# Two MLPs behind a retention layer: the state's product in 64x64 tiles, decays at the outputs, small loads on ScalarE's queue, one output bank in halves

## The chip, the cores and the metric

The kernel runs on one core of a Trainium2 chip. Its time is the device time of one execution in microseconds. Three runs of the kernel before gave 575.33, 578.35 and 578.90 us; the median is 578.35 us. One execution was profiled; its own time was 576.97 us.

## The reference

The program has three stages. First a retention layer over 2 sequences of 768 positions with 8 heads of 64 features, then an MLP with a rational activation, then an MLP with SiLU. Both MLPs take 1536 rows of 512 features through 2048 hidden features.

```python
gamma = 1.0 - 2.0 ** (-5.0 - np.arange(H))          # one decay per head
state = np.zeros((B, H, D, D))
for t in range(S):
    state = gamma * state + einsum('bhd,bhe->bhde', k[:, :, t], v[:, :, t])
    y[:, :, t] = scale * einsum('bhd,bhde->bhe', q[:, :, t], state)
x = y.transpose(0, 2, 1, 3).reshape(B * S, H * D)   # 1536 x 512
h = x @ w_in;   x = (P(h) / (Q(h) + 1e-6)) @ w_out  # P cubic in h, Q from |h| and h*h
h = x @ w_in2;  out = (h * sigmoid(h)) @ w_out2
```

## The kernel before, in words

**Retention in chunks.** The 1536 positions are cut into 12 chunks of 128: chunk c is piece c // 2 of sequence c % 2. A chunk has four parts on TensorE. The scores (line 472) are 8 products kT by qT with 64 rows of contraction, into two PSUM banks. VectorE masks each bank into SBUF (`am`, one 128x512 instruction a bank). The product of the masked scores with v (line 509) is 8 products with 64 output partitions. For the ten chunks that have a predecessor, the product of the state with the queries (line 519) is 4 products of 128x128: the state `bd` holds two heads of a pair in the two diagonal 64x64 blocks, the other two blocks are zero. Chunks 0 to 9 also add k by v to the state (line 497). All these operands are plain fp32, and the trace shows two records for one such product.

**Decays.** VectorE or GpSimd scales v by a falling decay (`vn`), and q by a rising one (`qT` by `gq`, line 467; `gq` is `up0` times a rate per piece). So the output of a chunk leaves PSUM as it is: ScalarE copies it to `xh`, VectorE subtracts to `xl`.

**MLPs.** Every fp32 matrix is carried as a high and a low half in fp32r (`xh` and `xl`, `ih`/`il` for w_in, `oh`/`ol` for w_out, `gh`/`gl` for the activations), and each product is three products of 128x512. A step is one block of 128 hidden features for a group of 512 rows: 12 products into a bank `h0`, `h1`, `a0` or `a1` (line 556), the activation on ScalarE and VectorE, the split into `gh` and `gl`, and 12 products into the four banks `acc0` to `acc3` (line 609). Weights come in 512 KB pieces (`raw`), which ScalarE and VectorE turn into fp32 (`wt`) and split. For one pair of groups of the second MLP seven products stand for eight (line 772). The end is 240 products of line 609 in a row for the last group; then ScalarE copies each `acc` bank to SBUF and SyncE sends it out (lines 644 and 654).

**Order.** The whole program is a list of operations with their dependencies (class `Flow`). The order in which each engine gets them is a table, `ORDER`, packed in a string. The functions fix the operations, buffers and banks; the table fixes the sequence on TensorE (PE), VectorE (DVE), ScalarE (ACT), GpSimd (POOL) and on SyncE's queue (SP). An instruction waits for the semaphores of what it depends on, and everything behind it on its engine waits too.

Of the kernel before, what the change touches and what calls it, by code (L numbers as in the profile page):

```python
# [11 lines left out]
F32 = mybir.dt.float32  # L12
# [11 lines left out]
R = {"gqd": 0, 'lw': -463.92, 'T0': 689.59, 'tau0': 13.93, 'tau1': 122.19, 'c0': -129.63, 'dc': 67.51, 'conv': 39.61, 'half': 427.29, 'absl': -34.77, 'raw': 455.03, 'ret': 752.06, 'spl': -417.39, 'hi': 301.24, 'lo': 31.56, 'inn': -277.93, 'later': -32.81, 'split': -554.53, 'out': 359.39, 'evac': -363.13, 'qload': -20.08, 'scl': 238.79, 'sc': 858.37, 'am': -44.15, 'gr': 112.48, 'av': -547.62, 'bd': 198.47, 'xh': -201.14, 'xl': 110.32, 'glp': 48, 'lop1': 24, 'lop2': 30, 'scp': 4, 'ps': 17, 'ksc': 103.89, 'qa': -467.29, 'ka': 0, 'late': 20, 'mid': 4, 'pev': -317.29, 'pld': -385.01, 'cg': -489.85, 'wm': 11, 'mk': 26.43, 'ck': 21.3, 'g2': (1, 0, 2), 'ch0': 269.21, 'ch1': -102.81, 'ch2': 64.3, 'ch3': 22.33, 'ch4': -52.46, 'ch5': 5.42, 'ch6': -78.23, 'ch7': 237.84, 'ch8': 90.06, 'ch9': -61.88, 'ch10': -106.39, 'ch11': -212.52, 'ru0': 218.22, 'lu0': -107.8, 'ru1': 40.68, 'lu1': -106.06, 'ru2': 91.09, 'lu2': 146.01, 'ru3': -37.17, 'lu3': -39.51, 'rhalf': 125.38, 'wsum': 20.0, 'kd': 4, 'hb': 20, 'turned': ()}  # L24
# [7 lines left out]
    'c-jrtW5W<;7XaXMA3xc(W!r1DW!tvB7Ps88ZQHhOn+wa@;+FNk|Ka*@eGdY0AvUB3ggEdW1OUhg=|CX?7^DRT2ZDr<2XaFOhzwC75hR9akOVTpkB',  # L32
    '}MSLoz4{Ng+DKgBVZ(qCj#;0Wl#fq=YPx7mh<INCnv-7UY8(@DuzDsUbg9hcu8K%0fXX068Ehl!Ka32Y!HDP#8`?8K?kt;T)8QlTZv!K_RFO^`JO',
    'hg)>kDN<)2U0T-YWG=T1K7S2OaxCXW0Pq+w;pgB~9>rf3Y!xi`oB88^V5E{cxh#6YK9cTkh;56KZW>66-Llt-rci|R%fKSjC9zvAR4t{~D5IOt~v',
    'BO8`0<l8W&<f&&-{1>$g-4Jew1&s<1lmInxB-8|CHNKYLkH*touMN<g+Y)s`~%$}dguxFAYO<czCtf}24%u$h!LK{_n|kufR``~qJ{6mD@Yi=!9a',
# [4 lines left out]
    'RaOjVPRp|8Fq&~FgWZ9Gs0Tf8)k)lVSi|f2f~JMF<c0j!mqd}Yz_y*<!~i5!>eI6tbuD`9sC(uVQbt1_rvvYBRmK<!^7|>ObUlW2W*4Q@o~5no`k',  # L40
    '1iE6ffp@b9oOY=gG=Hf#!A@O?NO{t3^*v2ZeMhb`e<_yybHZfKAD;Y0Woo`)UqBK#F*hBM)F*bB$QK5+aPPK1}?RX7ql;+OC>+zxlbx3Cjt<1RP=',
    'X9Hj)jKJ6b=l4DSj*;<R_%|R%!KfGw-vq)1!Eg@F#poCV6Jbk?iATe!5DS09*w_^lVq#2!NpT@A!n+|8#zDro7!Q+Sa!i5qFbgim|3XSkg_*G%rp',
    '7dw6|-XwT!M!n8!Da-oiHut#2;`icE`?m5DH*H{0;>RVJ`d;bK`PciAym77RAE20yAPdoR7tDJ;ui(_$L;}O1KIS!!am<d9Wmw!pc}0GvETOg6r@',
# [935 lines left out]
```

## Time and profile before

| | us |
|---|---|
| median of 3 runs (lowest, highest) | 578.35 (575.33, 578.90) |
| profiled execution, its own time | 576.97 |
| span of its trace | 575.2 |
| PE busy | 565.8 |
| VectorE busy | 432.8 |
| ScalarE busy | 405.9 |
| GpSimd busy | 184.5 |

The span is from the first to the last instruction of the trace. "Busy" is the time in which at least one instruction of the engine ran. PE's granted clock is given as a share of full speed (1.00 is 2.4 GHz, 0.50 is 1.2 GHz; a value between the two is a mean over a stretch). "DMA share" is the mean busy share of the 16 DMA engines. A `<-` behind an idle time names what ended it.

### The profile page before, as it was taken

How to read it: one execution, taken by the hardware profiler on the slowest of the kernel's cores; microseconds unless marked ns; L12 is line 12 of the kernel's file. 1: busy time of each engine (PE TensorE's matmuls, PEld its weight loads, DVE VectorE, ACT ScalarE, POOL GpSimd, SP SyncE). 2: the span in 40 equal slices, each digit the busy share in tenths (PEclk: the TensorE clock that was granted, in tenths of full speed). 3: DMA queues.
4: the chain of work that ended last, by engine and by line, in shares of the span. 5: the costliest groups of instructions: out<-in, count | busy, mean ns of one | idle time of the engine just before them, and what ended most of it. 6: DMA issues, size and time to landing. Idle time of an engine off the chain costs nothing.

```text
span 575.2 us, 8252 instructions
## 1 busy us (share of the span) xinstructions
PE 565.8 (98%) x2912; PEld 466.3 (81%) x2912; DVE 432.8 (75%) x680; ACT 405.9 (71%) x698; POOL 184.5 (32%) x148
## 2 busy tenths in 40 slices
PE   8989999999999999999999999999999999999997
PEld 7867878888788888888888888888888888888885
DVE  5888889788988898797988567578887888673341
ACT  2688889889999879788999877786544545424332
POOL 2556574633454634263373743310000000000000
PEclk8989999999999999999999999999999999999999
DMA  8996843632321321012134668864323422117811
GB/s 257 358 362 228 300 170 97 216 116 86 128 89 59 111 71 58 19 37 92 68 134 154 211 210 291 263 209 165 128 93 108 148 73 94 54 41 227 257 61 74
DMA packets 41441, 85.05 MB, mean 148 GB/s; under 512 B 4150, under 2 KB 4278, under 8 KB 41400
## 3 DMA queue, kind: packets, MB, share of 16 engines
q1 hardware_dynamic: 41400, 84.52, 43.1%
q8 instruction: 23, 0.38, 0.3%
q14 instruction: 18, 0.15, 0.1%
HBM read 63.53 MB, written 20.97 MB: 147 GB/s over the span
## 4 chain that ended last, share of the span: by engine, by line
PE 90%; DVE 3%; ACT 3%; DMA 2%; issue 1%; SPq 0%; POOL 0%; ACTq 0%
PE acc L609 42%; PE h L556 18%; PE a L556 10%; PE h L772 7%; PE a L772 7%; PE a L472 2%; DMA kn<-in_k_dram 1%; PE a L509 1%; PE a L519 1%; ACT h L331 1%; DVE s L346 1%; PE a L497 1%; DMA qT<-in_qt_dram 1%; DVE u L346 1%; PE h L509 1%
## 5 line engine op out<-in xcount | busy, mean ns | idle before, releaser
L339 POOL TENSOR_TENSOR gl<-s,gh 128x512 fp32r<-128x512 f32 x48 | 63.6, 1328 | 109.5 <-ACT gh L331 70.7
L609 PE MATMUL acc<-gh,oh 128*128 128x512 f32 x192 | 75.5, 393 | 0.0
L609 PE MATMUL acc<-gl,oh 128*128 128x512 f32 x192 | 74.8, 389 | 0.0
L609 PE MATMUL acc<-gh,ol 128*128 128x512 f32 x192 | 74.8, 389 | 0.0
L609 PE MATMUL acc<-oh,gh 128*128 128x512 f32 x192 | 74.7, 389 | 0.0
L609 PE MATMUL acc<-ol,gh 128*128 128x512 f32 x192 | 74.7, 389 | 0.0
L609 PE MATMUL acc<-oh,gl 128*128 128x512 f32 x192 | 74.7, 389 | 0.0
L556 PE MATMUL h<-xh,ih 128*128 128x512 f32 x168 | 66.2, 394 | 0.1
L556 PE MATMUL h<-xl,ih 128*128 128x512 f32 x168 | 65.5, 390 | 0.0
L556 PE MATMUL h<-xh,il 128*128 128x512 f32 x168 | 65.5, 390 | 0.0
L346 DVE SCALAR_TENSOR_TENSOR wt<-wt,raw 128x512 int32<-128x512 int32 x64 | 49.2, 778 | 17.1 <-ACT raw L331 13.2
L417 POOL TENSOR_TENSOR ol<-wt,oh 128x512 fp32r<-128x512 f32 x36 | 48.3, 1349 | 30.8 <-ACT oh L412 26.1
L417 POOL TENSOR_TENSOR il<-wt,ih 128x512 fp32r<-128x512 f32 x36 | 47.6, 1332 | 32.3 <-ACT ih L412 30.3
L331 ACT ACTIVATE raw<-raw,par 128x512 int32<-128x512 uint32 x64 | 48.3, 762 | 3.3 <-DMA raw<-in_moe_w_in_dram 1.7
L346 DVE SCALAR_TENSOR_TENSOR s<-s,par,h 128x512 f32<-128x512 f32 x65 | 48.2, 745 | 2.5 <-ACT w L331 1.0
L331 ACT ACTIVATE gh<-s 128x512 fp32r<-128x512 f32 x56 | 35.0, 626 | 14.2 <-DVE s L346 7.4
L331 ACT ACTIVATE wt<-raw 128x512 f32<-128x512 f32 x64 | 42.4, 664 | 3.0 <-DMA raw<-in_moe_w_out_dram 1.8
L609 PEld LDWEIGHTS acc<-gh,oh 128*128 128x128 f32 x192 | 36.0, 188 | 7.9
L609 PEld LDWEIGHTS acc<-gl,oh 128*128 128x128 f32 x192 | 36.0, 188 | 7.6
L609 PEld LDWEIGHTS acc<-oh,gl 128*128 128x128 f32 x192 | 36.0, 188 | 7.5
L609 PEld LDWEIGHTS acc<-ol,gh 128*128 128x128 f32 x192 | 36.0, 188 | 7.5
L609 PEld LDWEIGHTS acc<-oh,gh 128*128 128x128 f32 x192 | 36.0, 188 | 7.4
(263 smaller groups left out, 1301.0 us busy)
## 6 DMA issues: line engine op xcount, KB each, us to landing
raw<-in_moe_w_in_dram SPq DMA_DIRECT2D x32, 512.0 KB, 4.7
raw<-in_moe_w_out_dram SPq DMA_DIRECT2D x32, 512.0 KB, 4.7
spill<-wt SPq DMA_DIRECT2D x48, 256.0 KB, 4.5
wt<-spill SPq DMA_DIRECT2D x48, 256.0 KB, 2.9
vn<-in_v_dram SPq DMA_DIRECT2D x12, 256.0 KB, 4.2
qT<-in_qt_dram SPq DMA_DIRECT2D x12, 256.0 KB, 4.5
kT<-in_kt_dram SPq DMA_DIRECT2D x12, 256.0 KB, 4.6
kn<-in_k_dram SPq DMA_DIRECT2D x10, 256.0 KB, 4.6
```

Of the source, the lines that this page charges most:

```text
L331: lambda: nc.scalar.activation(out=out_, in_=in_, func=func, **kw),
L339: op(eng, dur, rank, lambda: e.tensor_tensor(out=out_, in0=in0, in1=in1, op=alu), reads, writes, port)
L346: lambda: nc.vector.scalar_tensor_tensor(out=out_, in0=in0, scalar=scalar, in1=in1, op0=op0, op1=op1),
L417: e.tensor_tensor(out=sl.t[nm + "l"][:, us], in0=wt.t, in1=sl.t[nm + "h"][:, us].bitcast(F32), op=ALU.subtract)
L472: nc.tensor.matmul(heads(sb_[j].t)[:, hp, :], kT.t[js, hp, :], qT.t[js, hp, :], start=True, stop=True)
L497: nc.tensor.matmul(st.t[j * D : (j + 1) * D, hp * D : (hp + 1) * D], kn.t[:, 2 * hp + j, :], vn.t[:, 2 * hp + j, :], start=(hp == 0), stop ...
L509: nc.tensor.matmul(heads(xo.t)[j * D : (j + 1) * D, hp, :], vn.t[:, 2 * hp + j, :], heads(am[j].t)[:, hp, :], start=(hp == 0), stop=not mo ...
L519: nc.tensor.matmul(heads(xo.t)[:, hp, :], old.t[:, hp, :], qT.t[:, hp, :], start=False, stop=True, skip_group_check=True,)
L556: nc.tensor.matmul(h.t, sl.t[w][:, ws], x[g].t[:, c, :], start=(n == 0), stop=(n == 3 * KD - 1))
L609: nc.tensor.matmul(a.t, a1, a2, start=(first and n == 0), stop=(last and n == 2))
L772: nc.tensor.matmul(b_.t, w[0](c, wlo), x[0](c, xlo), start=(start and n == 0), stop=(n == 5), skip_group_check=True)
```

## The change

- **State's product.** `bd` becomes 128x4x64 without zero blocks: four heads lie in partitions 0 to 63 and four in 64 to 127. The product with the queries is 8 products of 64x64 by 128 (line 523), which go round the four quarters of the array. Half of the queries lie in the other half of the partitions than their state, so GpSimd copies these into `qm` (two 64x256 copies a chunk, line 457). The two row halves write two banks, which are the chunk's own score banks.
- **Decays at the outputs.** q is no longer scaled. The output is multiplied by `up0` (piece 0) or `gq` when VectorE takes it out of PSUM into `xf` (one 128x512 instruction, or two of 128x256 for chunks with a state); ScalarE copies `xf` to `xh`. The subtraction to `xl` is VectorE's for chunks 0 to 3 and GpSimd's after that. The addition to the state is one 128x256 instruction instead of two of 64x256.
- **Small transfers.** The constants and parameters are loaded from ScalarE's queue (`beside`, 4 loads) instead of SyncE's (5 loads). Some memsets move from VectorE to GpSimd, two on GpSimd go, the identity goes, and the warming products at the start are 6 instead of 11.
- **Last bank in halves.** For the last group of the second MLP, the last step of bank `acc3` is two times three products of 256 columns, each half with its own copy and transfer.
- **Order.** `ORDER` is a new table, and the chunks are entered in the list of operations in four places instead of one; so banks and buffers can be shared in another sequence.

```diff
-R = {"gqd": 0, ..., 'wm': 11, ...}
+R = {"xp": 4, "vd": (0, 1, 2, 3), "early": ((0, 7), (2, 8), (3, 9), (4, 12)), "gqd": 0, ..., 'wm': 6, ...}
...
-    bd = [Buf(f"bd{r}", [P, HP, P], F32, at) for r in range(2)]
+    bd = [Buf(f"bd{r}", [P, HP, D], F32, at) for r in range(2)]
+    xfs = Turns("xf", 2, [P, GT], F32, at)
+    qms = Turns("qm", 2, [P, 2, P], F32, at)
-    gqs = Turns("gq", 2, [P, HP, P], F32, at)
+    gqs = Turns("gq", 1, [P, HP, P], F32, at)
...
+    def beside(rank, out_, in_, writes):
+        op("act", 0.42, rank, lambda: nc.scalar.dma_start(out=out_, in_=in_), [], writes)
...
+        if more:
+            qm = qms()
+            for r in range(2):
+                rs, js = slice(r * D, (r + 1) * D), slice((1 - r) * D, (2 - r) * D)
+                def move(out_=qm.t[rs, :, :], in_=qT.t[js, 2 * r : 2 * r + 2, :]):
+                    nc.gpsimd.tensor_copy(out=out_, in_=in_)
+                op("pool", 0.31, rank, move, [qT], [qm] if r == 0 else [qm.low])
...
-        tt("dve" if c < R["scp"] else "pool", rank - R["scl"], qT.t[:], qT.t[:], up, ALU.mult, [gq], [qT], port=more)
...
+        def place(hp, j):
+            x = xo[hp // 2 % len(xo)]
+            return heads(x.t)[j * D : (j + 1) * D, hp % 2 if len(xo) == 2 else hp, :]
...
             if more:
-                for hp in range(HP):
-                    nc.tensor.matmul(heads(xo.t)[:, hp, :], old.t[:, hp, :], qT.t[:, hp, :], ...)
+                for a in range(2):
+                    for r, j in ((0, 0), (1, 1), (0, 1), (1, 0)):
+                        hp, rs = 2 * r + a, slice(r * D, (r + 1) * D)
+                        x = qT.t[rs, hp, :] if r == j else qm.t[rs, a, :]
+                        nc.tensor.matmul(place(hp, j), state.t[rs, 2 * a + j, :], x, start=False, stop=True, skip_group_check=True)
...
-        act(rank + R["xh"], hi, heads(xo.t), AF.Copy, [xo], xh[g].chunk[o], True)
-        tt("dve", rank + R["xl"], lo, heads(xo.t), hi.bitcast(F32), ALU.subtract, [xo, *xh[g].chunk[o]], xl[g].chunk[o], port=False)
+        for n, x in enumerate(xo):
+            ks = slice(2 * n, 2 * n + 2) if more else slice(0, KD)
+            wide = 2 if more else KD
+            tt("dve", rank + R["xh"], whole[:, ks, :], heads(x.t)[:, 0:wide, :], shared[ci].t[:, ks, :], ALU.mult, [x, shared[ci]], [full], n=wide * P, port=False)
+        act(rank + R["xh"], hi, whole, AF.Copy, [full], xh[g].chunk[o])
+        tt("dve" if c < R["xp"] else "pool", rank + R["xl"], lo, whole, hi.bitcast(F32), ALU.subtract, [full, *xh[g].chunk[o]], xl[g].chunk[o])
...
+    def ends(now, g, sl, wr, cs, gh, gl, a):
+        for half in range(2):
+            hs = slice(half * GT // 2, (half + 1) * GT // 2)
...
+            op("pe", 0.36, now + R["out"], mm_end, ..., [c])
+            op("act", 0.263, now + R["evac"], lambda hs=hs: nc.scalar.activation(out=o.t[:, hs], in_=a.t[:, hs], func=AF.Copy, scale=0.5), [c], [to])
+            op("sync", 0.4, now + R["evac"], lambda hs=hs: nc.sync.dma_start(out=out[r0 : r0 + P, hs], in_=o.t[:, hs]), [to], [])
...
+            if last and l == 1 and g == gb and m == 3:
+                ends(now, g, sl, wr, cs, gh, gl, a)
+                continue
```

SyncE's queue at the start of the program, before (a name and a number are a buffer; `vn` is v, `kn` is k, both with positions in the partitions; `qT` and `kT` have features there; 88 KB `cst` holds the decays):

```order
L365 DMA vn_200<-in_v_dram 128x512
L365 DMA vn_201<-in_v_dram 128x512
L365 DMA cst<-in_consts_dram 128x176
L365 DMA qT_203<-in_qt_dram 128x512
L365 DMA t_177<-in_consts_dram 1x512
L365 DMA t_176<-in_consts_dram 1x512
L365 DMA qT_204<-in_qt_dram 128x512
L365 DMA kT_206<-in_kt_dram 128x512
L365 DMA kT_207<-in_kt_dram 128x512
L365 DMA pin<-in_moe_b_dram 1x2
L365 DMA pin<-in_moe_a_dram 1x4
L365 DMA kn_197<-in_k_dram 128x512
```

and after the change:

```order
L370 DMA qT_204<-in_qt_dram 128x512
L370 DMA kT_207<-in_kt_dram 128x512
L370 DMA vn_201<-in_v_dram 128x512
L370 DMA vn_199<-in_v_dram 128x512
L370 DMA raw_159<-in_moe_w_in_dram 128x2x512
L370 DMA vn_200<-in_v_dram 128x512
L370 DMA kT_208<-in_kt_dram 128x512
L370 DMA qT_205<-in_qt_dram 128x512
L370 DMA kT_207<-in_kt_dram 128x512
L370 DMA kn_196<-in_k_dram 128x512
```

q and k of chunk 0 now come first, the small loads are gone to ScalarE's queue (where `cst` is first), and a 512 KB piece of w_in comes fifth, ahead of k.

TensorE around the end of chunk 6, before (`a0`, `a1`, `h0` and `acc` are PSUM banks; line 497 adds to the state, 472 makes scores, 509 takes the masked scores, 519 the state):

```order
L497 MATMUL a0_184<-vn_2_202,kn_2_199 64x64 x8
L472 MATMUL a0_184<-qT_0_203,kT_0_206 128x128
...
L497 MATMUL a0_184<-vn_0_200,kn_0_197 64x64 x8
L509 MATMUL a1_185<-am0_212,vn_0_200 64x128
...
L519 MATMUL a1_185<-qT_0_203,bd0_195 128x128 x4
L556 MATMUL h0_190<-xh0_69,ih1_79 128x512
```

and after the change (494, 510, 523 and 560 are the lines that 497, 509, 519 and 556 were):

```order
L494 MATMUL acc2_187<-vn_0_199,kn_0_196 64x64 x8
L494 MATMUL acc3_188<-vn_2_201,kn_2_198 64x64 x8
L510 MATMUL a0_183<-am0_214,vn_0_199 64x128
...
L510 MATMUL a1_184<-am0_214,vn_0_199 64x128
...
L523 MATMUL a0_183<-qT_0_204,bd0_194 64x128
L523 MATMUL a1_184<-qT_0_204,bd0_194 64x128
L523 MATMUL a0_183<-qm_0_209,bd0_194 64x128
L523 MATMUL a1_184<-qm_0_209,bd0_194 64x128
...
L560 MATMUL h0_189<-xh0_68,ih1_78 128x512
```

Before, everything around chunk 6 goes through the banks `a0` and `a1`; now the additions to the state have `acc2` and `acc3`, which are still free there. In both, 24 products of the first MLP step pair and the chunks 0 to 6 lie ahead of the last row, and chunks 7 to 11 behind it.

TensorE at the very end, after the change (each bank's row stands for its last products):

```order
L609 MATMUL acc_188<-oh_84,gh_179 128x256
L609 MATMUL acc_188<-ol_85,gh_179 128x256
L609 MATMUL acc_188<-oh_84,gl_182 128x256
...
L637 MATMUL acc_187<-oh_84,gh_179 128x512
L637 MATMUL acc_187<-ol_85,gh_179 128x512
L637 MATMUL acc_187<-oh_84,gl_182 128x512
L637 MATMUL acc_185<-oh_84,gh_179 128x512
L637 MATMUL acc_185<-ol_85,gh_179 128x512
L637 MATMUL acc_185<-oh_84,gl_182 128x512
```

`acc_188` is bank `acc3`, the one in halves. Between its second half and the end stand 18 products of 512 columns; the bank that ends last is `acc0` (`acc_185`), whole, as it was before.

## Rows read from the trace of the kernel before

**Rows 1.** page part 1, busy us (share of span) and instructions of each engine

```profile
PE 565.8 (98%) x2912; PEld 466.3 (81%) x2912; DVE 432.8 (75%) x680; ACT 405.9 (71%) x698; POOL 184.5 (32%) x148
```

**Rows 2.** windows; PE, PEld, DVE, ACT, POOL busy us (instructions), PEclk, DMA share, GB/s

```profile
44.40:571.60 527.20, 527.03 (x2484) 432.96 (x2482) 398.46 (x621) 378.86 (x651) 164.81 (x126) 1.00 0.40 134
5.00:41.30 36.30, 32.19 (x387) 27.07 (x387) 30.75 (x53) 22.08 (x41) 17.18 (x16) 0.94 0.98 354
...
140.00:160.00 20.00, 19.87 (x88) 16.10 (x87) 17.46 (x25) 19.05 (x34) 7.45 (x6) 1.00 0.27 94
```

**Rows 3.** windows, same columns, around the start

```profile
35.00:40.00 5.00, 3.32 (x50) 2.73 (x44) 4.59 (x8) 3.94 (x8) 3.46 (x3) 1.00 1.04 402
40.00:45.00 5.00, 4.18 (x42) 3.84 (x43) 4.89 (x9) 4.97 (x10) 3.21 (x4) 0.66 0.42 163
```

**Rows 4.** timeline 40:45: start us, us, engine, line, tile, form, count

```profile
40.04 1.28 DVE L339 TENSOR_TENSOR am<-a,causal 128x512 f32<-128x512 f32 x2
...
41.70 1.94 PE L509 MATMUL a<-am,vn 128*64 128x128 f32 x16
...
43.58 1.16 PE L519 MATMUL a<-qT,bd 128*128 128x128 f32 x8
...
44.49 0.47 PE L556 MATMUL h<-xh,ih 128*128 128x512 f32 x1
```

**Rows 5.** chain of waits: start us, us, what (chunk 8, and the end)

```profile
84.53 1.02 PE a L509 x16
85.55 1.09 PE a L519 x8
...
516.49 54.41 PE acc L609 x240
```

**Rows 6.** PE groups by form: busy us, mean ns, idle

```profile
L519 PE MATMUL a<-qT,bd 128*128 128x128 f32 x64 | 9.3, 288 | 0.0
```

**Rows 7.** timeline: weight loads and products of 64 columns

```profile
26.27 0.55 PEld L497 LDWEIGHTS a<-vn,kn 128*64 128x64 f32 x16 [0.70 <-DMA kn<-in_k_dram]
...
26.79 0.64 PE L497 MATMUL h<-vn,kn 128*64 128x64 f32 x16
...
34.36 0.85 PEld L509 LDWEIGHTS a<-am,vn 128*64 128x64 f32 x16 [0.35 <-issue]
```

**Rows 8.** timeline 0:12, SyncE's issues and VectorE's first work

```profile
0.74 0.86 SPq L365 DMA_DIRECT2D vn<-in_v_dram  x2
1.64 0.42 SPq L365 DMA_DIRECT2D cst<-in_consts_dram  x1
...
5.00 0.69 DVE L339 TENSOR_TENSOR vn<-vn,cst 128x512 f32<-128x512 f32 x1 [3.57 <-DMA cst<-in_consts_dram]
...
8.19 1.16 PE L472 MATMUL a<-qT,kT 64*128 64x128 f32 x16 [0.78 <-DMA kn<-in_k_dram]
...
29.66 0.44 SPq L365 DMA_DIRECT2D kn<-in_k_dram  x1
```

**Rows 9.** VectorE and GpSimd groups by form: busy us, mean ns, idle

```profile
L339 DVE TENSOR_TENSOR xl<-a,xh 128x512 fp32r<-128x512 f32 x8 | 5.5, 683 | 0.1
...
L339 DVE TENSOR_TENSOR bd<-a,bd 64x256 f32<-64x256 f32 x12 | 5.0, 420 | 1.2 <-PE a L497 1.1
...
L346 DVE SCALAR_TENSOR_TENSOR wt<-wt,raw 128x512 int32<-128x512 int32 x64 | 49.2, 778 | 17.1 <-ACT raw L331 13.2 <-ACT wt L331 3.8
...
L339 POOL TENSOR_TENSOR qT<-qT,gq 128x512 f32<-128x512 f32 x8 | 10.3, 1284 | 9.2 <-DMA qT<-in_qt_dram 9.2
...
L834 POOL MEMSET bd<- 128x512 f32 x2 | 1.0, 524 | 0.3 <-POOLq L956 0.3
```

**Rows 10.** page part 6, DMA issues: count, KB each, median us to landing

```profile
kn<-in_k_dram SPq DMA_DIRECT2D x10, 256.0 KB, 4.6
```

**Rows 11.** timeline, the end of the program

```profile
571.60 0.60 ACT L644 ACTIVATE u<-acc 128x512 f32<-128x512 f32 x1
...
572.23 0.33 SPq L654 DMA_DIRECT2D out_dram<-u  x1
```

More of the change, by code (lines that the diff above doesn't have):

```diff
@@ L509, in outs @@
                     nc.tensor.matmul(
-                        heads(xo.t)[j * D : (j + 1) * D, hp, :],
+                        place(hp, j),
                         vn.t[:, 2 * hp + j, :],
                         heads(am[j].t)[:, hp, :],
-                        start=(hp == 0),
+                        start=(hp % 2 == 0 if more else hp == 0),
                         stop=not more,
@@ L528, in attention @@
         if grows:
             op("pe", 0.6, rank + R["gr"], grow, [kn, vn], [st])
-        op("pe", 1.94 if more else 0.98, rank + R["av"], outs, [vn, *am] + ([old, qT] if more else []), [xo])
+        op("pe", 1.5 if more else 0.98, rank + R["av"], outs, [vn, *am] + ([state, qT, qm, qm.low] if more else []), xo)
         if grows:
-            sv = st.t[:, 0 : HP * D].rearrange("p (a e) -> p a e", a=HP)
-            for j in range(2):
-                js = slice(j * D, (j + 1) * D)
-                if not more:
-                    act(rank + R["bd"], new.t[js, :, js], sv[js], AF.Copy, [st], [new], True, n=HP * D)
-                else:
-                    tt("dve", rank + R["bd"], new.t[js, :, js], sv[js], new.t[js, :, js], ALU.add, [st], [new], n=HP * D, port=False)
@@ L539, in attention @@
[L539 to L542 removed]
+            sv, to = st.t[:, 0 : HP * D], state.t[:].rearrange("p a e -> p (a e)")
+            if not more:
+                act(rank + R["bd"], to, sv, AF.Copy, [st], [state], True, n=HP * D)
+            else:
+                tt("dve", rank + R["bd"], to, sv, to, ALU.add, [st], [state], n=HP * D, port=False)
@@ L608, in mm_out @@
                 for n, (a1, a2) in enumerate(ops):
-                    nc.tensor.matmul(a.t, a1, a2, start=(first and n == 0), stop=(last and n == 2))
+                    apart = l == 1 and g == gb and m == 3
+                    nc.tensor.matmul(
+                        a.t, a1, a2, start=(first and n == 0), stop=((last or apart) and n == 2), skip_group_check=apart
+                    )
             op("pe", 0.68, now + R["out"], mm_out, [sl.cells["oh", j], sl.cells["ol", j], gh, gl], [a])
@@ L850, in relate @@
             nc.tensor.matmul(
[L851 removed]
+                bank["acc2"].t[j * D : (j + 1) * D, NGAM : NGAM + NCI * KD],
                 ones.t[:, 0:D],
@@ L897, in switch @@
             slots[r].make(tail, r)
-    op("host", 0.0, 0.0, switch, [], at_cells + [x for r in range(RING, RING + LATE) for x in slots[r].all])
+    attend(range(early[0][1]))
     s = 0
@@ L917, in retention_two_mlps @@
             continue
+        for nth, (at_u, upto) in enumerate(early[1:]):
+            if u == at_u:
+                attend(range(early[nth][1], upto))
+        if u == early[-1][0]:
+            at_cells = [up0, rates] + xfs.bufs + bd + ams + [x for y in (kns, vns, qTs, kTs, gqs, qms) for x in y.bufs] + [x.low for x in qms.bufs]
+            op("host", 0.0, 0.0, switch, [], at_cells + [x for r in range(RING, RING + LATE) for x in slots[r].all])
         for n, j in enumerate((0, 1) if p % 2 == 0 else (1, 0)):
```

211 lines of the change are left out of this document (100 added, 111 removed).

## The prediction

> **What bounds the kernel now.** I read the page's busy shares first, then busy time by windows, then the timeline around the place where the windows change character, and the chain of waits last. PE is busy 98% of the span [rows 1]. By windows this is two programs. From 44.4 us, where the third MLP step starts [rows 4], to 571.6 us PE is busy 527.03 of 527.20 us at full clock [rows 2]: after 44.4 us only work taken from PE, or a new stall, moves the end. Before that PE waits for others. From 5 to 41.3 us VectorE is busy 30.75 of 36.3 us with 53 instructions, and the DMA engines have a share of 0.98 [rows 2], 1.04 just before the end of it [rows 3]. What ends this stretch is VectorE's masks of chunk 6, done at 41.32, then PE's products with them (1.94 us) and with the state (1.16) up to 44.49 [rows 4]; PE's granted clock is 0.66 there [rows 3], a mean between its two levels. Behind the last product come 3.6 us of output: the copy at 571.60 and the transfer issued at 572.23 [rows 11], to the span's end at 575.2.
>
> So there are three terms: when the saturated stretch begins, how much PE work is in it, and the tail. The working is against the profiled execution, 576.97 us, which lies 1.4 below the median of 578.35; I carry the difference over to the median.
>
> **Term 1: the start.** VectorE's first useful instruction runs at 5.00 after 3.57 us without work, and waits for `cst`, which SyncE issues at 1.64 behind two loads of v [rows 8]. From issue to use that is 3.4 us. Issued first on ScalarE's queue, near 0.74, it would be there at 4.1 or a little sooner, since no load is ahead of it: 0.9 to 1.5 us, I take 1.2. From there to the masks of chunk 6 the order has 50 instructions on VectorE where it had 55 with two memsets. Out go four scalings of q and two subtractions to `xl` (0.683 each [rows 9], 4.1 us), five additions to the state (0.42 [rows 9], 2.1 us) and one step of the activation (0.7). In come two multiplications of 512 columns (1.4), six of 256 (0.42 each by the 256-column row [rows 9], 2.5) and one more `wt` (0.78 [rows 9]). That is 2.2 us less, with some 0.1 more for a memset: 2.3. VectorE is busy 85% of the stretch, so I let the masks be earlier by 1.2 + 2.3 = 3.5 us, at 37.8. Behind them stand the two products of chunk 6, the second shorter by 0.5 (term 2). That is 4.0 us. PE should also run them at a clock nearer 1.00, since it no longer waits for the bank `a0` just before: of the 0.9 us that the first product took over its 1.02 elsewhere [rows 4, 5] I take half. Sum: **4.4 us**, saturated from 40.1 instead of 44.5.
>
> Can the loads keep up? Up to the last k that these chunks need, 41 units of 256 KB were asked for, and 44 are now, because weights come sooner. That k was issued at 29.66 [rows 8] and a load of k lands 4.6 us after its issue [rows 10]: 34.3. Three units at 402 GB/s [rows 3] are 2.0 us: 36.3. Adding to the state for chunks 6 and 5, the masked product and the state's product take another 0.6 + 0.6 + 1.0 + 0.6 on PE, which gives 39.1. It fits, and it is the floor: the start cannot give much more than 5.4 us. GpSimd has 17.18 us of work in 36.3 [rows 2]. It loses three scalings of 1.28 [rows 9] up to there and two memsets of 0.52, and gains about three subtractions (much like the scaling) and ten copies. No row shows such a copy. It has half the columns of the memset and of the scaling: 0.26 to 0.64 each; I take 0.3, as it reads one operand only, and cover it by GpSimd's idle time: 3 to 6 us beside 19. At the price of 0.64 and with that cover gone the start loses up to 3 us.
>
> **Term 2: PE work in the saturated stretch.** The records of a state's product last 0.288 us each and overlap [rows 6], so a block is read from the chain: 1.09 us [rows 5]. Ten such blocks go, ten of eight small products come. No row has 64x64 tiles. From below: a block with the same streaming, eight products of 64 columns in two halves of the array, 16 loads of 64 columns each, takes 0.55 to 0.64 [rows 7]. From above: 1.09, no gain, if only two quarters work at a time; worse, if one does (rival 4). I take 0.6, since the row of the same streaming has the same number of weight loads. Saved: 0.49 a block. Five blocks lie in the stretch (chunks 7 to 11): **2.4 us**, between 0 and 2.7. The score products, masked products and additions to the state are as they were, and so are the 2,256 products of 512 columns, except that three become six of 256: nothing (54.41 us for 240 [rows 5] is 0.227 each, against 0.213 for 512 columns at 2.4 GHz, so three more starts cost 0.04).
>
> GpSimd's new subtractions and copies in this stretch take the place of five scalings of 1.28; it is busy 164.81 of 527.2 us [rows 2]. VectorE's sums are equal within 1 us, ScalarE's within 0.5. The four loads now on ScalarE's queue cost it about 0.4 each in the first 3 us, when it has nothing to do. Covers: its work in the first 40 us is far from full.
>
> **Term 3: the tail.** The halved bank is not the last: 18 products of 512 columns stand behind it, 4.1 us by [rows 5], and the bank that ends last is whole, as before. A whole copy (0.60) and a 256 KB transfer stand at the end as they did [rows 11]. **0 us**; had the last bank been the halved one, it would have been about 0.3.
>
> Sum: 4.4 + 2.4 + 0 = 6.8 us. 576.97 becomes 570.2, and against the median of 578.35 I forecast **571.5 us**.
>
> **A rule against it.** For 64 columns the weight loads could set the pace. [rows 7] has both: 16 loads of 64 columns take 0.55 us in front of narrow products and 0.85 in front of wide ones, where the products themselves take 1.02. The Trainium skill ("TensorE: Matmul & The Clock Gate", section on LDWEIGHTS) gives a load's time as its columns at 1.2 GHz, that is 53 ns for 64 columns; 16 one after another would be 0.85 us, and by that price term 2 would be 1.2 us and not 2.4. The row of 0.55 shows that loads into different parts of the array need not follow each other in that way, so the measurement decides for 0.6.
>
> **Rivals.**
> 1. *The loads or GpSimd's queue set the start.* For it: the DMA share of 1.04 and the three units more; GpSimd's copies stand in its queue ahead of the low halves of the weights and wait for q. Against: the floor of 39.1. The start then gives 0 to 1.5 us: 578.35 - 2.4 - 0.7 = 575.2.
> 2. *The weight loads pace the small products.* A block then takes 0.85 or more [rows 7], up to 1.02. Five blocks give 0.8 instead of 2.4 and the start 0.3 less: 573.4. The skill's sentence above is this rule.
> 3. *ScalarE gives it back later.* It is busy 19.05 of 20 us between 140 and 160, where PE has lost 0.13 [rows 2]. If PE comes 2.4 us sooner by less work of its own, and ScalarE, which has no less, cannot follow, term 2 is lost there: 573.9. Against: ScalarE starts earlier with the rest, by term 1.
> 4. *Slower: the quarters run one at a time.* One half-array pair now takes 1.02 for eight products [rows 5], two at a time; one at a time eight would take some 1.9, 0.8 more than the block that went. The five late chunks then cost 4.0 instead of giving 2.4, and the chunks 4 to 6, which are PE's at the end of the start, 3.9 (1.3 each), with more at a clock below 1.00: 571.5 + 6.4 + 3.9 + 1 = 583. It is slower than before from a block of about 1.6 us on. Against: column halves (line 509 [rows 5]) and row halves (the scores, 1.16 for eight [rows 8]) each run two at a time already.
>
> **Chances.** Forecast 0.57, its own range 568.5 to 574.5; rival 1: 0.18; rival 2: 0.09; rival 3: 0.10; rival 4: 0.06. The range for 8 in 10 is 567.5 to 577: below, the floor of the loads (5.4) with 2.7 and the half width of the runs (1.8); above, rival 1 with the same width. About 1% (5.8 us) is what a measurement of this kernel tells from no change. Faster by more needs 572.6 or less: three quarters and more of the forecast, a third of rival 2, a fifth of rival 3: 0.52. Slower by over 1% is rival 4 and mishaps of the new order: 0.06. Within: 0.42.
>
> **What would show it.** In the trace after: the first step of PE without gaps at 39 to 41.5 (term 1), the masks of chunk 6 about 3.5 earlier; line 523's eight products in 0.55 to 0.7 (1.0 or more: rival 2; 1.6 or more: rival 4); copies of 0.3 to 0.4 on GpSimd; 3.6 us between the last product and the end. Wrong would be: idle PE after 45 us, a clock near 0.5 for more than 5 us in the first 40 because the warming is shorter, or a start that hangs on a load.

## The result, and the profile after

The changed kernel takes **572.02 us** (median of 7 runs, 571.48 to 573.56), the kernel before 577.41 (7 runs); the ratio is 0.9913, with an interval of 0.9892 to 0.9934. That is 5.4 us or 0.9% less, inside the 1% that I had called no change, and 0.5 us above the forecast of 571.5. The profiled execution took 571.89 us with a span of 570.2, against 576.97 and 575.2. The four new runs of the kernel before have moved its median from 578.35 to 577.41.

Busy time by windows of the changed kernel: first the same stretches as in [rows 2], to the masks of chunk 6, to the start of the gapless stretch, and to the last product; then two early windows for the clock.

```profile
core 0: us, PE busy (x) PEld busy (x) DVE busy (x) ACT busy (x) POOL busy (x), PEclk, DMA share, GB/s
5.00:39.73 34.73, 29.98 (x414) 24.54 (x412) 28.25 (x50) 22.59 (x42) 15.98 (x21) 0.90 0.93 330
39.73:41.46 1.73, 1.68 (x31) 1.34 (x31) 1.70 (x4) 1.73 (x5) 1.73 (x2) 1.00 0.96 294
41.46:566.52 525.06, 524.91 (x2524) 430.67 (x2523) 405.76 (x623) 382.80 (x653) 179.72 (x141) 1.00 0.42 136
5.00:10.00 5.00, 3.28 (x36) 2.83 (x34) 2.83 (x7) 2.01 (x5) 0.00 (x0) 0.75 0.92 302
10.00:15.00 5.00, 4.24 (x48) 3.54 (x46) 3.79 (x6) 1.84 (x6) 2.19 (x4) 0.57 0.92 337
```

The start and the work can be read off. The gapless stretch begins at 41.46 instead of 44.49: **term 1 is 3.0 us** (forecast 4.4). It lasts 525.06 instead of 527.08, from 44.49 to the end of the last product at 571.57: **term 2 is 2.0** (forecast 2.4). From the last product to the end of the span are 3.7 us, against 3.6: **term 3 is 0**, as forecast. The spans differ by 5.0.

The chain of waits of the changed kernel (start, us, what): three waits for transfers and then the first gapless step; and a late chunk with its value product, its state product and what follows.

```profile
5.32 5.70 DMA qT<-in_qt_dram
...
13.27 4.17 DMA kT<-in_kt_dram
...
23.07 5.64 DMA raw<-in_moe_w_in_dram
...
41.46 2.95 PE h L560 x12
...
79.84 1.02 PE a L510 x16
80.86 0.60 PE a L523 x16
81.46 0.61 PE h L494 x16
```

Line 523 is the state's product: 0.60 us a block where line 519 took 1.09 [rows 5]. This is the value that I took; neither a block of 0.85 (rival 2) nor of 1.6 (rival 4) is there.

Part of the start, by the timeline of each kernel: the keys that SyncE issues, and what stands at the two ends. First before, where line 472 is the scores and line 556 the first block of the first MLP:

```profile
9.16 1.78 PE L472 MATMUL acc<-qT,kT 64*128 64x128 f32 x16
10.96 0.33 SPq L365 DMA_DIRECT2D kT<-in_kt_dram  x1
27.36 0.50 PE L556 MATMUL h<-xh,ih 128*128 128x512 f32 x1
```

Then after, where the same are lines 468 and 560. The bracket is the wait ahead of an instruction, with what ended it.

```profile
3.91 0.23 DVE L864 TENSOR_SCALAR causal<-cst 128x128 f32<-128x128 f32 x1 [3.91 <-DMA cst<-in_consts_dram]
5.58 1.34 DVE L344 TENSOR_TENSOR vn<-vn,cst 128x512 f32<-128x512 f32 x2 [1.44 <-DMA vn<-in_v_dram]
11.15 2.08 PE L468 MATMUL acc<-qT,kT 64*128 64x128 f32 x16 [0.76 <-DMA qT<-in_qt_dram]
13.27 0.33 SPq L370 DMA_DIRECT2D kT<-in_kt_dram  x1
17.48 1.16 PE L468 MATMUL a<-qT,kT 64*128 64x128 f32 x16 [1.04 <-DMA kT<-in_kt_dram]
25.77 0.50 PE L560 MATMUL h<-xh,ih 128*128 128x512 f32 x1
```

VectorE's first instruction comes 1.1 us sooner, at 3.91 instead of 5.00. But it is a small one, which builds the mask. The scaling of v, which stood at 5.00 before [rows 8], now waits 1.44 us more for v, whose load stands behind q and k, and starts at 5.58. Chunk 1's scores start 2.0 us later, at 11.15 instead of 9.16, and the keys of chunk 3 are issued 2.3 later, at 13.27 instead of 10.96. In both kernels that issue comes where chunk 1's scores end (9.16 + 1.78, and 11.15 + 2.08): the two buffers for keys are taken, and chunk 3 gets the one that chunk 1 leaves. The first block of the MLP is 1.6 us earlier all the same. From there to the masks of chunk 6 are 13.96 us in both kernels (27.36 to 41.32, 25.77 to 39.73). The rest of term 1, 1.4 us, is chunk 6's products: 3.17 us before, at a clock of 0.66 [rows 3], and 1.73 after, at 1.00.

### The profile page after: what moved, and what is told of

It reads as the page before. It is cut to its first block, busy times and chain, and to the rows that moved or that the text cites. A ratio compares the mean times of both kernels' runs of the same rounds, so it can differ in the third digit from the quotient of the medians.

```text
span 570.2 us, 8451 instructions
## 1 busy us (share of the span) xinstructions
PE 560.5 (98%) x2985; PEld 459.5 (81%) x2985; DVE 435.9 (76%) x676; ACT 408.7 (72%) x697; POOL 198.0 (35%) x170
## 4 chain that ended last, share of the span: by engine, by line
PE 91%; DMA 3%; DVE 3%; ACT 2%; issue 1%; SPq 0%; DVEq 0%; ACTq 0%
PE acc L637 45%; PE h L560 18%; PE a L560 11%; PE h L802 7%; PE a L802 7%; PE a L510 1%; DMA qT<-in_qt_dram 1%; DMA raw<-in_moe_w_in_dram 1%; PE a L468 1%; DMA kT<-in_kt_dram 1%; PE a L523 1%; DVE am L344 1%; DMA cst<-in_consts_dram 1%; PE h L494 0%; ACT s L336 0%
## 5 line engine op out<-in xcount | busy, mean ns | idle before, releaser
L344 POOL TENSOR_TENSOR gl<-s,gh 128x512 fp32r<-128x512 f32 x48 | 64.9, 1352 | 79.3 <-ACT gh L336 60.3
L351 DVE SCALAR_TENSOR_TENSOR wt<-wt,raw 128x512 int32<-128x512 int32 x64 | 54.2, 853 | 12.7 <-ACT wt L336 6.8
L426 POOL TENSOR_TENSOR ol<-wt,oh 128x512 fp32r<-128x512 f32 x36 | 51.2, 1425 | 34.6 <-ACT oh L421 31.8
L426 POOL TENSOR_TENSOR il<-wt,ih 128x512 fp32r<-128x512 f32 x36 | 49.5, 1381 | 23.8 <-ACT ih L421 19.3
L637 PEld LDWEIGHTS acc<-gh,ol 128*128 128x128 f32 x192 | 36.1, 188 | 7.2
```

What stands on the lines that cost most here:

```text
L344: op(eng, dur, rank, lambda: e.tensor_tensor(out=out_, in0=in0, in1=in1, op=alu), reads, writes, port)
L351: lambda: nc.vector.scalar_tensor_tensor(out=out_, in0=in0, scalar=scalar, in1=in1, op0=op0, op1=op1),
L426: e.tensor_tensor(out=sl.t[nm + "l"][:, us], in0=wt.t, in1=sl.t[nm + "h"][:, us].bitcast(F32), op=ALU.subtract)
L637: nc.tensor.matmul(a.t, a1, a2, start=(first and n == 0), stop=((last or apart) and n == 2), skip_group_check=apart)
```

## The experiments

All are the changed kernel with one edit, the last two with several. Each ratio is to runs of the kernel before on the same chip, in turn with the variant's (medians 576.9 to 577.6). The first four kernels ran on one chip, the next four on another, the next three on a third, the last on a fourth. Runs of one kernel differ by 0.5 to 3.7 us, so less than a microsecond is read from the traces and not from the medians. But each kernel has one profile, and these scatter as well: the second and the fourth kernel below hardly touch the beginning, and their gapless stretch starts at 41.95 and 43.08, where the changed kernel's profile has 41.46. One start that moves by half a microsecond shows nothing by itself.

### The state's product over all 128 rows

```diff
-x = qT.t[rs, hp, :] if r == j else qm.t[rs, a, :]
-nc.tensor.matmul(place(hp, j), state.t[rs, 2 * a + j, :], x, ...)
+nc.tensor.matmul(place(hp, j), state.t[:, 2 * a + j, :], qT.t[:, hp, :], ...)
```

> The changed kernel with its state product over all 128 rows again (eight products of 128x64 weights by 128 columns, each adding the other head's terms to the output; the copies on GpSimd stay). Theory: the second term of the prediction comes from the quarters of TensorE working side by side. Then the block goes from 0.60 to about 1.02 us, as the value product's blocks of the same shape; five of the ten blocks lie after the start of the gapless stretch, so the stretch is 5 x 0.42 = 2.1 us longer (525.1 to about 527.2) and the start 0.4 to 0.8 later: 574.3 to 575.0 by the median. Rival: the stretch became shorter for another reason (the decay's place, fewer products); then the block is longer but the stretch stays within 0.5 us of 525.1 and the time is 572.0 to 572.8.

It took 573.34 us, ratio 0.9940 (0.9920 to 0.9960), 1.1 to 1.3 above the three other kernels on that chip. The chain of waits of this run, at the same chunk as above:

```profile
80.51 1.02 PE a L510 x16
81.53 0.87 PE a L523 x16
82.40 0.46 PE h L494 x16
```

The time is 0.7 us under the theory's range. The theory is right in kind: the block grows. But it grows by 0.27 us, not by 0.42, and the block behind it (k by v, line 494) shrinks by 0.15. Both have the same reason. Weights of 128 rows and 64 columns are also the shape of the blocks on either side, and a block that follows its own shape is 0.15 us shorter: 0.87 here against 1.02 for line 510, which has as many products of the same size and follows another shape; 0.46 against 0.61 for line 494. Five blocks of 0.27 less three of 0.15 are 0.9 us, and the stretch is 525.97, 0.9 longer (that alone would lie in its scatter, see below; the blocks' lengths are the evidence). If the quarters' block pays the same 0.15 on entry, its own work is 0.45 and the wide block's 0.87: the 0.42 that I expected is there, and two changes of shape saved take most of it back.

### Both products of a quarter in a row

```diff
-for a in range(2):
-    for r, j in ((0, 0), (1, 1), (0, 1), (1, 0)):
+for r, j in ((0, 0), (1, 1), (0, 1), (1, 0)):
+    for a in range(2):
```

> The changed kernel with the eight products of a state block in another order: both products of one 64x64 quarter one after the other, then the next quarter. Theory: the two row halves take products independently, about 0.11 us apart in each half, whatever the columns; then the block is 0.65 to 0.75 us (five steps in place of four) and the time 572.0 to 573.0. Rival: a quarter must end one product before it takes the next, or the queue lets nothing past; then the block is 1.0 us or more, the stretch 2.0 us longer, and the time 574 or more.

572.28 us, 0.9925 (0.9904 to 0.9946). The chain of this run:

```profile
108.30 1.02 PE a L510 x16
109.33 0.62 PE a L523 x16
109.94 2.96 PE h L560 x12
```

0.62 against 0.60: even less than the theory's 0.65 to 0.75. Of the two orders tried neither matters much, and neither lets the quarters run one at a time, as rival 4 has it.

### No copies on GpSimd

```diff
-nc.gpsimd.tensor_copy(out=out_, in_=in_)
+pass
...
-x = qT.t[rs, hp, :] if r == j else qm.t[rs, a, :]
+x = qT.t[rs, hp, :]
```

> The changed kernel without the copies on GpSimd: every quarter reads the query rows that lie in its own row half, so two of four read another head's queries. 20 copies of 0.44 us go. Theory: the copies lie in GpSimd's idle time and beside it, so that the start of the gapless stretch moves by at most 0.5 us, and the stretch by at most 0.3: 571.3 to 572.3. Rival: the copies hold up GpSimd, which is busy all the time from 35 to 50 us, and with it VectorE, whose rebuilding of weights takes 853 ns where it took 778; then the start comes 1.0 us or more earlier and the time is 571.0 or less, with the weights' rebuilding back near 780 ns.

572.10 us, 0.9921 (0.9901 to 0.9941); the stretch starts at 41.66. The groups of the changed kernel, and of this run (count, busy us, mean ns, idle before):

```profile
L351 DVE SCALAR_TENSOR_TENSOR wt<-wt,raw 128x512 int32<-128x512 int32 x64 | 54.2, 853 | 12.7 <-ACT wt L336 6.8 <-ACT raw L336 5.8
L457 POOL COPY qm<-qT 64x256 f32<-64x256 f32 x20 | 8.7, 436 | 6.8 <-DMA qT<-in_qt_dram 5.8
```

```profile
L351 DVE SCALAR_TENSOR_TENSOR wt<-wt,raw 128x512 int32<-128x512 int32 x64 | 54.6, 859 | 13.1 <-ACT wt L336 7.2 <-ACT raw L336 5.9
```

A copy takes 0.44 us, not my 0.3, and all 20 are hidden. Nor do they slow VectorE: its rebuilding of weights is as slow without them (859 ns, before 778 [rows 9]). What slows it is open.

### The halved bank last

```diff
+for n, to in [(2338, 2331), (2341, 2338), (2339, 2341), (2342, 2339), (2340, 2342), (2343, 2340)]:
+    # the halves' products, copies and stores, each behind the next, at the end of the order
```

> The changed kernel with the halved bank moved to the end of the program, behind the last whole bank on TensorE, ScalarE and SyncE. Theory of the prediction's third term: the halving brought nothing because the halved bank isn't the last; as the last one it shortens what follows the last product from 3.7 to about 3.4 us: 571.6 to 571.8. Rival: the tail is the fixed time of an output transfer, whatever its size; then it stays 3.6 to 3.7 us and the time at 572.0.

572.09 us, 0.9916 (0.9896 to 0.9935). The timeline of this run's end (its program ends at 572.8, in the slowest of its four runs):

```profile
568.43 0.60 ACT L674 ACTIVATE u<-acc 128x512 f32<-128x512 f32 x1
568.83 0.28 PE L609 MATMUL acc<-oh,gl 128*128 128x256 f32 x1
569.14 0.66 ACT L612 ACTIVATE s<-acc 128x256 f32<-128x256 f32 x2
569.55 0.83 SPq L613 DMA_DIRECT2D out_dram<-s  x2
```

From the last product (569.11) to the end are 3.7 us, as before: the rival's number. Its reason, a fixed time of a transfer, isn't shown: ScalarE is still at the whole bank's copy when the first half is ready, and there are two transfers to issue where there was one. So the halving brings nothing in either place, and my 0.3 "had the last bank been the halved one" was wrong as well.

### TensorE kept busy from the beginning

```diff
+extra = {24: (4, "h1"), 10: (3, "h1"), 28: (2, "h0")}   # behind which operation, how many, which bank
 for o in flow.order():
     o.emit()
+    if o.index in extra:
+        idle(*extra[o.index])      # products of 128x128 zeros
```

> The changed kernel with nine more 128x128 warming products in TensorE's waits before chunk 1: four behind chunk 0's scores, three ahead of its value products, two behind them. Theory: what term 1 of the prediction lacks (3.0 us measured, 4.4 forecast) is TensorE's slow pace from 5 to 13 us, where blocks take 2.0 us that take 1.0 to 1.1 later; kept at work it runs at full pace, chunk 0's value products take about 1.0 in place of 1.98 us and chunk 1's scores about 1.1 in place of 2.08, and the gapless stretch starts 0.7 to 1.4 us earlier than 41.5 to 42: 570.6 to 571.4 by the median. Rival: loads set it; chunk 1's scores still wait for their queries until 11 us, the blocks get faster and the start stays within 0.4 us: 571.8 to 572.4.

573.27 us, 0.9924 (0.9908 to 0.9940). The timeline of PE in this run (L954 is the added products):

```profile
6.01 2.08 PE L468 MATMUL a<-qT,kT 64*128 64x128 f32 x16
8.01 2.07 PE L954 MATMUL h<-u 128*128 128x128 f32 x8
10.54 0.94 PE L954 MATMUL h<-u 128*128 128x128 f32 x6
11.46 1.09 PE L510 MATMUL h<-am,vn 128*64 128x128 f32 x16
13.13 1.16 PE L468 MATMUL acc<-qT,kT 64*128 64x128 f32 x16
```

The pace doubled near 10.5 us and chunk 1's scores took 1.16 instead of 2.08. But the added products had delayed them by 2 us, so they ended at 14.3 instead of 13.25. The start came at 42.20: the rival. The slow pace can't be bought off this way; whether it costs anything is the next question.

### The first weights behind the queries and keys of chunks 1 and 2

```diff
-SP: ..., vn, raw (512 KB), vn, kT, qT, kT, kn, qT, qT, ...
+SP: ..., vn, vn, kT, qT, kT, kn, qT, raw (512 KB), qT, ...
```

> The changed kernel with one transfer moved: the first 512 KB of weights is issued behind chunk 1's and chunk 2's queries and keys in place of fifth, and the three instructions that rebuild weights from it stand later on ScalarE and VectorE. Theory: the big transfer in front of chunk 1's keys and queries is what term 1 lacks; without it they land 1.0 to 1.4 us earlier, chunk 1's scores start near 9.8 in place of 11.15, and the gapless stretch 0.8 to 1.4 us earlier: 570.6 to 571.2. Rival: the weights are needed just as soon; what chunk 1 gains is lost when ScalarE and VectorE wait for weights between 15 and 25 us, and the start moves by less than 0.4 us: 571.7 to 572.4.

572.73 us, 0.9927 (0.9902 to 0.9952), start 41.60: the rival by its start, but not for its reason. (The four kernels on this chip lie together at 572.7 to 573.3, somewhat above the ranges I gave; I go by their starts.) The timeline:

```profile
9.54 1.98 PE L510 MATMUL h<-am,vn 128*64 128x128 f32 x16 [0.94 <-DVE am L344]
11.45 2.08 PE L468 MATMUL acc<-qT,kT 64*128 64x128 f32 x16
13.60 0.33 SPq L370 DMA_DIRECT2D kT<-in_kt_dram  x1
```

Chunk 1's scores no longer wait for a load. They wait for PE, which runs at half pace until 13.5 us in this run, and start no sooner. But three profiles in which chunk 0's scores are as slow (2.08 us) and this load stands where it did, among them those of the two kernels that hardly touch the beginning, have them at 11.45 to 11.59 too. So this run shows that late queries and slow products end at about the same place, and not what the load costs where chunk 0's scores take 1.16 us, as in the changed kernel's profile.

### Two subtractions from VectorE to GpSimd

```diff
-tt("dve" if c < R["xp"] else "pool", rank + R["xl"], lo, whole, ...)
+tt("dve" if 2 <= c < R["xp"] else "pool", rank + R["xl"], lo, whole, ...)
```

> The changed kernel with the low parts of chunks 0 and 1 on GpSimd in place of VectorE: 2 x 0.68 us less on VectorE before the gapless stretch, 2 x 1.4 more on GpSimd, which is idle there. Theory: VectorE's work sets the start (it is busy all the time from 35 us to chunk 6's masks); the start comes 0.7 to 1.4 us earlier: 570.6 to 571.3. Rival: VectorE waits for 7 us in all before that, and the work taken away turns into more waiting for transfers and for ScalarE: start within 0.4 us, 571.7 to 572.4.

572.98 us, 0.9912 (0.9891 to 0.9933), start 41.44, first block of the MLP at 26.06: the rival. 1.36 us less work on VectorE ahead of that block bought nothing that this profile shows.

### The small transfers back on SyncE

```diff
-op("act", 0.42, rank, lambda: nc.scalar.dma_start(out=out_, in_=in_), [], writes)
+op("sync", 0.42, rank, lambda: nc.sync.dma_start(out=out_, in_=in_), [], writes)
```

> The changed kernel with its four small transfers back on SyncE's queue, at the same places in the program's order. Theory (the first part of term 1): on ScalarE's queue they gain 1.1 us, since they no longer stand between SyncE's large issues of 0.4 us each; back on SyncE chunk 0's scores start 0.8 to 1.3 us later than 5.16 and the gapless stretch 0.6 to 1.3 us later: 572.6 to 573.4. Rival: the start doesn't hang on chunk 0 (chunk 1's queries land when the queues have moved what stands ahead of them, whoever issues it): start within 0.4 us, 571.7 to 572.4.

572.88 us, 0.9916 (0.9891 to 0.9941), start 41.95, first block at 26.03. Chunk 0's scores start at 6.24 instead of 5.16, and that looks like the theory. But they take 2.08 us here, and in the seven other profiles where they are that slow they start at 6.00 to 6.14 with the small transfers on ScalarE's queue; only 0.1 to 0.2 us is the edit's. Chunk 1's start at 12.26, and by the first block no delay is left. The median would fit the theory, but so would those of the other kernels on that chip; the start is 0.5 later than in the changed kernel's profile and among those of its variants: rather the rival. VectorE's first instruction comes at 2.71 in this run, earlier still, for `cst` is first on SyncE's queue here; its scaling of v then waits until 6.84 for v. So the edit doesn't undo the first part of my term 1, and the time of that first instruction is nothing that the start hangs on.

Four edits ahead of the first block, in both directions, and it came between 25.8 and 26.8 us in all nine profiles so far. The common place ahead of it is the issue of chunk 3's keys, at 12.9 to 14.4. Three more runs test it and the row behind it.

### One rebuilding of weights behind chunk 6's masks

```diff
 DVE: u, t,
-     wt, am, am,
+     am, am, wt,
      h, s, ...
```

> The changed kernel with one rebuilding of weights (0.68 us on VectorE, which stood right ahead of chunk 6's masks) behind those masks, the transfer that waits for its buffer and the rounding that reads it moved back with it. Theory after eight runs: the gapless stretch starts 15.2 to 15.7 us after the first block of the first layer, whatever is done before, because from there VectorE works through a fixed row of instructions that ends with chunk 6's masks; one of 0.68 us less ahead of them moves the start by 0.6 to 0.7 us: about 14.6 to 15.1 us behind the first block, 571.3 to 571.8. Rival: TensorE's own work (24 products, two score blocks, a value and a state block) or GpSimd's low part of the weights holds the start; then it stays at 15.2 to 15.7 and the time at 572.0 to 572.5.

572.36 us, 0.9911 (0.9895 to 0.9927), and 15.9 us from the first block to the first gapless product: the theory fell, and the trace says why. VectorE and PE in this run:

```profile
40.23 0.70 DVE L351 SCALAR_TENSOR_TENSOR h<-t,h 128x512 f32<-128x512 f32 x1
40.96 0.75 DVE L351 SCALAR_TENSOR_TENSOR s<-s,par,h 128x512 f32<-128x512 f32 x1
41.86 0.47 PE L560 MATMUL h<-xh,ih 128*128 128x512 f32 x1 [0.61 <-ACT raw L336]
```

The next block of the MLP writes bank `h0`. Until 41.7 VectorE's `s` still reads it, two instructions behind the masks; ScalarE, which the view names, reads no bank there. So the row on VectorE has two ends, the masks and the gate of step 0, and moving work between them moves neither's sum. They lie within 0.3 us of each other in the changed kernel too. (In the nine profiles before this one the distance from the first block to the start is 15.3 to 16.3 us, and not the 15.2 to 15.7 of the theory.)

### Chunk 1's keys in an idle tile

```diff
-kT = load(0.0, kTs, kt[b, ci])
+if c == 1:
+    kT = ew["t"].bufs[1]
+    dma(rank - R["qload"], 0.66, kT.t, kt[b, ci], [], [kT])
+else:
+    kT = load(0.0, kTs, kt[b, ci])
+keys = heads(kT.t) if c == 1 else kT.t
...   (the scores read keys in place of kT.t)
```

> The changed kernel with chunk 1's keys in a tile that is idle until the first layer, so that chunk 3's keys need not wait for chunk 1's scores (their transfer is issued at 12.9 to 14.4 us in nine profiles, the moment these scores end, and holds up all of SyncE's queue behind it). Theory: this wait is what turns slow early products, late queries and the small transfers into the same start; without it chunk 3's scores start 0.8 to 1.5 us earlier than 17.5 and the first block of the first layer 0.6 to 1.2 earlier than 25.8 to 26.8; start 0.6 to 1.2 earlier, 571.0 to 571.6. Rival: the transfers are at their rate (0.85 to 0.95 of their time busy from 5 to 20 us), or VectorE is, so the keys land as late, or the first block waits for other things: within 0.4 us, 571.8 to 572.4.

**571.38 us**, 0.9899 (0.9884 to 0.9915), the lowest median of all, though its interval overlaps that of the changed kernel. The timeline, then the chain's first gapless step:

```profile
9.40 0.33 SPq L370 DMA_DIRECT2D kT<-in_kt_dram  x1
11.48 2.08 PE L473 MATMUL acc<-qT,t 64*128 64x128 f32 x16
14.25 0.33 SPq L370 DMA_DIRECT2D vn<-in_v_dram  x1
16.25 1.16 PE L473 MATMUL a<-qT,kT 64*128 64x128 f32 x16
24.34 0.50 PE L565 MATMUL h<-xh,ih 128*128 128x512 f32 x1
```

```profile
40.20 2.96 PE h L565 x12
```

Chunk 3's keys are issued 3.9 us earlier, its scores start 1.2 earlier, the first block 1.4 and the gapless stretch 1.3, with chunk 1's scores as late and as slow as in the runs above. In the three profiles with this edit (this one and the next two) the stretch starts at 40.1 to 40.6 us, in the ten without it at 41.4 to 43.1: the wait for a key buffer held the start. It did so through the two loads that come earlier now, chunk 3's keys and a load of k (10.26 instead of 13.64), and not by holding up all of SyncE's queue: here the queue stops again, for a buffer of v, and issues that load at 14.25, where the changed kernel did so at 14.32.

### All three

The edits of the last two runs, and chunk 0's and 1's subtractions on GpSimd.

> The changed kernel with three edits: chunk 1's keys in the idle tile, one rebuilding of weights behind chunk 6's masks, the low parts of chunks 0 and 1 on GpSimd. Theory: the first lets TensorE and VectorE get at chunk 3 earlier, the third takes 1.36 us from VectorE where it is then full (20 to 25 us), the second shortens the row behind: first block near 24.8, start 1.5 to 2.0 us earlier than 41.5 to 42, 570.2 to 570.8. Rival: only the second counts: 571.3 to 571.8.

571.64 us, 0.9903 (0.9888 to 0.9917): first block at 24.56, the first gapless product at 40.13, behind a wait of 0.36 for `s`. Only one edit counts, as the rival has it, but it is the keys and not the masks.

### The rebuilding behind both ends

```diff
 DVE: u, t,
-     wt, am, am, h, s,
+     am, am, h, s, wt,
```

> The kernel with chunk 1's keys in the idle tile, and the one rebuilding of weights now behind both chunk 6's masks and the two instructions that end step 0's gate and so free bank h0 (in the run before it stood between them, and TensorE's first gapless product waited 0.36 to 0.61 us for that bank). Theory: the fixed row on VectorE ends with both, within 0.3 us of each other; with 0.68 us less ahead of both, the start is 0.5 to 0.7 us earlier than with the keys alone (40.2): 39.5 to 39.8, and the time 570.6 to 571.0. Rival: the weights that are rebuilt later, and the 512 KB that wait for their buffer, are wanted soon after, and the stretch gets as much longer: 571.2 to 571.6.

572.64 us, 0.9922 (0.9905 to 0.9939). The row from the first block to the first gapless product is 15.0 us (25.52 to 40.56) where it was 15.6 to 15.9 in the changed kernel and in the three runs above. That fits this part of the theory, but the shortest of the other profiles has 15.3. And the stretch is 526.3 us long, 0.7 longer than with the keys alone. VectorE now stands still in it for weights, which the moved transfer brings later, and TensorE is busy 18.55 of the 19 us from 41 to 60, where it was busy all 19 with the keys alone:

```profile
47.26 0.69 DVE L351 SCALAR_TENSOR_TENSOR wt<-wt,raw 128x512 int32<-128x512 int32 x1 [1.69 <-ACT wt L336]
```

That is the rival in kind, and 1.0 us past its range. Why the first block came at 25.52 here and not near 24.4, with the keys issued at 9.25, one profile can't tell; chunk 2's scores took 1.75 us in it and 1.16 in the run with the keys alone.

## Why the prediction was right, and where it wasn't

**The number.** 571.5 and 572.02 lie closer together than the terms do, and that is luck. I took 6.8 us from 578.35, the median of three runs; by seven runs that kernel takes 577.41, and the change is worth 5.4. So 0.9 of the 1.4 us by which my sum is too large don't show in the time. Two of the signs that I had called wrong are there as well: the start hangs on a load, and the clock was near 0.5 for more than 5 us (0.75 and 0.57 in the windows from 5 to 15 us make 6.8 us at 0.50, if the rest of them is at 1.00).

**Term 1 (4.4 forecast, 3.0 measured).** The step that failed is "VectorE is busy 85% of the stretch, so I let the masks be earlier by 1.2 + 2.3 = 3.5 us"; they are 1.6 earlier. Both amounts are there: VectorE's first instruction comes 1.1 sooner, and its work from there to the masks is 28.5 us (28.25 in the window above and 0.23 ahead of it) instead of 30.75 [rows 2]. But its waits in between grew by 1.8 us, from 5.55 to 7.34; the 1.44 for v, right behind the first instruction, is one of them. I read the share of busy time over 36 us as if the whole of it were one queue. It was two. Up to the first block of the MLP VectorE waits in turn for loads, ScalarE and PE, and the link that held it was chunk 3's keys, which wait for the buffer that chunk 1's scores leave. The edits to VectorE's work and to the small transfers moved the start by under 0.5 us, which is scatter; the buffer moved it by 1.3. From the first block to the masks are 13.96 us in both kernels, and VectorE is busy 12.06 of them, 12.44 before: nearly all of the work saved lay ahead of the block, where it turned into waiting. The change had also put 512 KB of weights ahead of chunk 1's queries and keys (before, the first such load is issued at 11.35); whether that delayed the link isn't shown, since TensorE's slow pace hid it in the run that moved the load. I had the row on the loads' rate (its floor of 39.1 holds) and none on which buffer a load waits for.

The other part of the term, 0.5 for the shorter product and half of the 0.9 for the clock, was too small: chunk 6's products take 1.73 us at full clock instead of 3.17 at 0.66, that is 1.4 instead of 0.95.

**Term 2 (2.4 forecast, 2.0 measured).** The block is 0.60 as forecast, but five blocks don't save five times 0.49. What I put at nothing is the price of a change of tile shape for what stands behind the block. Before, three of the five late blocks of line 519 stand right ahead of products of the MLP, which have the same 128x128 shape and lose next to nothing there; behind the quarters' block they lose 0.24 us. The chains of waits show it, first before and then after; elsewhere three products of the MLP take 0.68 us and twelve 2.72.

```profile
105.53 1.09 PE a L519 x8
106.62 0.70 PE acc L609 x3
```

```profile
108.77 0.60 PE a L523 x16
109.37 2.96 PE h L560 x12
...
134.32 2.72 PE h L560 x12
```

So two of the five chunks save 0.49, two some 0.27, and one 0.15 (there a k-by-v block had the value product behind it before, and that saved a change already): 1.7 us in all. The other 0.3 can't be told from scatter: in 13 profiles of the changed kernel and its variants the stretch is 525.0 to 526.3, and the kernel before has one profile. Of the 2,256 products that I counted in the stretch 24 lie ahead of it; nothing hangs on them.

The Trainium skill ("TensorE: Matmul & The Clock Gate", section on LDWEIGHTS) gives a price by which 16 loads one after another would be 0.85, an estimate; the trace differs, with 16 loads and their products in 0.60, and the measurement decides. The Trainium skill ("TensorEngine Tiling (Array Packing)", section Tiling Modes) says that different tiles take loads and products in parallel, and that a change of tiling mode drains the engine. The first agrees with 0.60. The second fits the 0.15 to 0.24 us that a change of shape costs here; that this time is a drain no run shows.

**Term 3 (0).** Right, and the run with the halved bank last shows that its place was not the reason.

**Rivals.** Rival 1 named the right kind of thing, a load, with too small a gain (0 to 1.5); what held was neither the DMA's rate nor GpSimd's queue but one load's wait for its buffer. Rivals 2 and 4 fell with the block of 0.60. Of rival 3 only 0.15 us of idle PE between 120 and 140 us is left, as much as the 0.13 before, 20 us later [rows 2]. The chances had the greater part on faster by over 1%. That hung on the 1.4 us of term 1.

## What to carry to other kernels

Before you turn saved work into saved time, find the instruction at which the stretch ends, go back from it buffer by buffer, and ask of every transfer on the way not only when it lands but what released its issue: a busy share of 85% hid a ring of two buffers, behind which four edits left no clear trace. Where two chains end within some tenths of a microsecond (masks and gate here), work taken off one of them buys nothing; off both it may, if what was moved isn't wanted soon after. And when a product is cut into other tiles, count the changes of tile shape with it, those of the products behind it too.

## What the runs showed of the hardware

- Going to another tile shape costs TensorE about 0.15 us: eight products with 128x64 weights by 128 columns take 1.02 us behind another shape and 0.87 behind their own, a k-by-v block 0.61 and 0.46. The MLP's 128x128 products lose 0.24 behind 64x64 tiles (twelve in 2.96 instead of 2.72) and 0.02 behind plain fp32 products of their own shape (three in 0.70 instead of 0.68).
- Four 64x64 quarters with plain fp32 run side by side: eight products, in 16 records, take 0.60 us, and 0.62 with both products of a quarter in a row. With 128x64 weights the same number of products takes 0.87.
- In the first 15 us TensorE's pace is one of two kinds. In the changed kernel's profile chunk 0's scores took 1.16 us, and the clock then fell (0.75, 0.57). In eight of the other twelve profiles they took 2.08, with a granted clock of 1.00 in the same rows, so the rows of the clock do not show every slow stretch; the time of a known block does. (In these eight traces the first record of the clock comes only at 10.5 to 16.4 us. In the run with the added products it comes at 10.5, and there their pace rose.)
